# Weight sums staged in place and over several steps, a cosine argument in turns, and earlier re-reads in an attention and two-layer feed-forward kernel

## Chip, cores and metric

The kernel runs on one core of one Trainium2 chip. The metric is device microseconds of one execution, and the median of a few executions is compared. The profiled execution is one more such execution, taken with the hardware profiler; the rows below are its rows.

## What is computed

An attention with a decay, then two feed-forward layers on 2304 tokens of width 512 (the weights arrive as 64-bit floats and are made into pairs of 32-bit parts on the chip):

```python
scores = scale * q @ k.T ; cum = cumsum(log(clip(f)))
scores = where(causal, -1e9, scores + cum[..., :, None] - cum[..., None, :])
x = softmax(scores) @ v                      # 32 heads, 576 x 64 each -> x: 2304 x 512
h = x @ w_in ; x = (h * cos(h)) @ w_out      # first layer, inner width 2048
g = x @ w_gate ; val = x @ w_val             # second layer, inner width 1536
out = (g / (1 + exp(-g)) * val) @ w_out2
```

## The kernel before

Four stages follow each other on the engines. **Attention** (to 191 us of the span) runs by a schedule written out by hand. **The first layer** (191 to 678 us) takes the tokens in 6 chunks of 384 and the inner width in 16 blocks of 128, 96 steps in all (the loop at L691). In a step, TensorE does 12 matmuls of 128x384 into a PSUM tile `h` (`mm_in`, L250) and then the 12 matmuls of `out1` (L613) for the block of two steps earlier. In between, `in1` makes h*cos(h): ScalarE rounds h/2pi+0.25 to an integer `n` (L586), VectorE takes n times 2pi from h in two operations (L590, L592), ScalarE takes the sine (L594), VectorE multiplies (L596), ScalarE casts the product to `gh` (L598) and VectorE takes the rest as `gl` (L116 by `subtract`). `out1` needs both. The order of all this within a step is the string `ORD1`: a digit is an operation of `in1` (5 and 6 are those of the step before), `o` is `out1`, `w` one operation of the conversion of a weight, and `c` one entry of the list `small`. Each engine runs its instructions strictly in the order written, and so does SyncE, which issues all DMAs.

In the same 96 steps the weights are converted. `w_load` (L153) reads a raw weight of 512 KB into one of WRB = 3 buffers `wraw`, `w_step` converts it in five operations (L169 on ScalarE, L171 to L177 on VectorE) into a tile `ta`, and the next raw load is issued behind the fifth. Weights of the first layer get two more operations (L191, L116). The 36 weights of the second layer are taken two at a time by `w_member`, 18 pairs in all: it puts twelve entries on `small`, which are four sums or differences on GpSimd (`tt`, L210, into the one buffer `sums`), and four times a cast to a high part on ScalarE (`high`, L226), a difference on GpSimd for the low part (`low`, L116) and a store of both parts to HBM (L230). High and low part share a tile `wst`, of which there are two. A `c` takes one entry, and where more than TAB2-2 = 2 converted weights are held, `w_step` takes entries off the list at once (L165) until they are fewer.

**The second layer's first half** (678 to 989 us) is done as seven products (a fast 2x2 scheme) per block q of the inner width and per token pass p: two groups of three blocks, three passes each (L878). In a block, `in2` does seven groups of 12 matmuls (L783); VectorE combines them (L676), and `silu` (L763 to L767) makes a 128x384 piece of g four times, once with VectorE and three times with GpSimd, and stores each with three DMAs of 64 KB. During the second block of a pass `x_sums` (L676 on `xb`) combines the inputs of the next pass on VectorE, and during the third `x_split` casts them. `x_read` (L661, four DMAs) re-reads them from HBM; it is called behind the first block of the pass.

**The second layer's second half** (989 to 1149 us) does the same with g: `g_load` (L811) reads it, `g_sums` combines it (GpSimd and VectorE), `g_split` casts it, and `out2` (L842) does seven groups of 18 matmuls for each of nine token tiles t. Tile t+1 is combined and cast during tile t. `g_load(1)` stands behind all reads of the weights (`u_read`, L666).

Of the kernel before, what the change touches and what calls it, by code (L numbers as in the profile page):

```python
# [26 lines left out]
CH = 384  # L27
# [10 lines left out]
TAB = 2  # L38
TAB2 = 4
CHAIN = 1  # L40
# [13 lines left out]
POS_OUT = {2: 0, 3: 1, 5: 2, 6: 3, 7: 4, 4: 5, 1: 6}  # L54
WRB = 3
ORD1 = "0152w634owwccc"
WQ = (3, 2)
# [8 lines left out]
INV2PI = float(1 / (2 * np.pi))  # L66
PI2_HI, PI2_LO = 6.28125, 0.0019353071795864769

# [30 lines left out]
def body(ctx: ExitStack, tc: tile.TileContext, qk, v, f, w_in, w_out, w_gate, w_val, w_out2, mask_c, ident_c, sel_c, out):  # L99
# [6 lines left out]
    x2 = [dram.tile([128, KD, CH], F32, name=f"x2_{k}") for k in range(NC)]  # L106
    w_u = [dram.tile([7, 128, 2, 512], F32, name=f"wu{u}") for u in range(9)]
    g_d = [dram.tile([4, 128, NQ, 128], F32, name=f"gd{t}") for t in range(NIT)]
    r_d = dram.tile([NPAIR, 10, 128], F32, name="r_d")
# [28 lines left out]
    small = []  # L138
    held = [0]

# [15 lines left out]
    def w_step(n, k):  # L156
# [6 lines left out]
        if k == 1:  # L163
            sp = stages[0] if n < SA else stages[1]
            while n >= SB and held[0] > TAB2 - 2:  # L165
                small.pop(0)()
            ta = wcur[n][1] = sp.tile([128, 512], I32, tag="ta", name="ta", bufs=TAB if n < SA else TAB2)
# [30 lines left out]
    def w_member(kind, q):  # L198

        b0, b1 = half.pop((kind, 2 * q)), half.pop((kind, 2 * q + 1))  # L200
        a0, a1, c0, c1 = b0[:, :256], b0[:, 256:], b1[:, :256], b1[:, 256:]
        box = {}
        ins = kind != "p"
        u, mem = (q, "gv".index(kind)) if ins else (NQ + q // 2, q % 2)

        def tt(o, a, b, op):
            if "s" not in box:
                box["s"] = stages[1].tile([128, 4, 256], F32, tag="sums", name="sums", bufs=1)
            a, b = (box["s"][:, x] if isinstance(x, int) else x for x in (a, b))
# [3 lines left out]
        for x in ((0, c0, c1, add), (2, a0, c0, sub), (1, c1, 2, sub), (3, a1, 1, sub)) if ins else \  # L213
                ((2, c1, a1, sub), (0, a1, a0, sub), (1, 2, a0, add), (3, c0, 1, sub)):
            small.append(lambda x=x: tt(*x))
# [346 lines left out]
    lctx = ExitStack()  # L562
    mp2 = lctx.enter_context(tc.tile_pool(name="mp2", bufs=2))
# [3 lines left out]
    stages[1] = rctx.enter_context(tc.tile_pool(name="stage2", bufs=WRB, side=SIDE_R))  # L567
    ps_h = hctx.enter_context(tc.tile_pool(name="ps_h", bufs=3, space=PSUM))

# [6 lines left out]
    def in1(c, j, k):  # L576

        if k == 0:
            h = ps_h.tile([128, 512], F32, tag="h", name="h")[:, :CH]
            mm_in(h, wt["i", j], xs[c])  # L580
            n = mp2.tile([128, CH], I32, tag="n", name="n")
            r = mp3.tile([128, CH], F32, tag="r", name="r")
            hnr[c, j] = h, n, r
        h, n, r = hnr[c, j][:3]
        if k == 1:
            ACT.activation(out=n, in_=h, func=AF.Copy, scale=INV2PI, bias=0.25)  # L586
        elif k == 2:
            a = ps_h.tile([128, 512], F32, tag="a", name="a", bufs=1)[:, :CH]
            hnr[c, j] += (a,)
# [41 lines left out]
    def w_next():  # L631

        n, k = wpos
        if n < len(order):
            w_step(n, k)
        elif n > len(order):
            return
        if k == 5 and n + 1 < len(order):
            w_step(n + 1, 1)
        if SA < n <= SB and k in (3, 4):  # L640
            w_step(n - 1, k + 3)
        if k == 5 and n + WRB < len(order):
            w_load(n + WRB)
        wpos[:] = (n + 1, 2) if k == 5 else (n, k + 1)
# [18 lines left out]
    def u_read(u, i):  # L663
        s, t = slot_tile([128, 2, 2, 256], F32R, "wu")
        wu[u, i] = s, t
        SP.dma_start(out=t.bitcast(F32).rearrange("p m h x -> p m (h x)"), in_=w_u[u][(POS_IN if u < NQ else POS_OUT)[i]])  # L666

# [23 lines left out]
    for i in range(NCH + LAG):  # L691
        if i < NCH:
# [9 lines left out]
            if i == 0:  # L702
                for n in range(WRB):
                    w_load(SA + n)
            if i == WS:
                w_step(SA, 1)
            left = WQ[wpos[0] >= SB and i % 2] if i >= WS else 0
            for k in ORD1:
                if k in "01234":
# [51 lines left out]
    def silu(e, C, g, p, q, blk):  # L761
# [46 lines left out]
    def g_load(t):  # L808
        GT[t] = [slot_tile([128, NQ, 128], F32, "gt") for _ in range(4)]
        for e in range(4):  # L810
            SP.dma_start(out=GT[t][e][1], in_=g_d[t][e])  # L811

# [65 lines left out]
    for st in range(NST):  # L878
        for p in range(NPASS):
            final = st == NST - 1 and p == NPASS - 1  # L880
            nxt = None if final else (p + 1) % NPASS
            for q in range(NQS * st, NQS * st + NQS):
# [13 lines left out]

                in2(p, q, after)
                if k == 0 and not final:
                    for e in range(4):
                        x_read(e, nxt)  # L900
                if k == 0 and p == 0 and st == 0:
                    jobs += [(u, i) for u in range(4, NQ) for i in PO]
            if st == NST - 1 and p == NPASS - 2:
                free.extend(xid.values())
                g_load(0)
                for e in range(3):
                    sums[e] = slot_tile([128, NQ, 128], F32, "gs")
# [74 lines left out]
```

## Time and profile before

| | us |
|---|---|
| median of 3 executions (lowest, highest) | 1150.89 (1150.29, 1151.24) |
| the profiled execution | 1150.39 |
| its span, first to last instruction | 1148.6 |
| TensorE matmul busy in it | 1028.7 (90%) |
| VectorE busy | 720.1 (63%) |
| ScalarE busy | 510.1 (44%) |
| GpSimd busy | 519.0 (45%) |

TensorE is the engine that the others feed. An idle stretch of another engine costs nothing by itself, so the table is read together with the waits of TensorE, and with what its matmuls take when it is not waiting. Its mean granted clock is 0.943 of full speed; the clock has two levels in these rows, 2.4 GHz and half of it.

### The profile page before, as it was taken

The numbers are of one execution on the slowest core, as the hardware profiler recorded it, in microseconds if no ns is written. First come the engines' busy times: TensorE is split into PE (matmuls) and PEld (weight loads), VectorE is DVE, ScalarE is ACT, GpSimd is POOL, SyncE is SP. The second block draws the span as 40 slices with busy tenths as digits, with TensorE's granted clock in tenths as the row PEclk, the third lists the DMA queues.
The fourth block names the chain that finished last, engine by engine and source line by source line (L and its number), as shares of the span: only waits on it lengthen the run. The fifth ranks groups of instructions, "written<-read, shape, count | busy, mean of one in ns | idle before, by whom it ended". The sixth has DMA issues, their size and how long they took to land. (4 is left out here: it accounts for less than half of the span.)

```text
span 1148.6 us, 18643 instructions
## 1 busy us (share of the span) xinstructions
PE 1028.7 (90%) x6728; PEld 977.6 (85%) x6728; DVE 720.1 (63%) x1398; ACT 510.1 (44%) x1112; POOL 519.0 (45%) x476
## 2 busy tenths in 40 slices
PE   7999998999888878878889998989698799869998
PEld 5888886999888778868888998989688799869998
DVE  5888885888776566747655744645445455456763
ACT  7888883555444344434434532322122231324342
POOL 3656553422544545454363104526263546445562
PEclk9999999999988989888889998989898999979999
DMA  5666754234545455544634773134742317944421
GB/s 189 199 178 210 211 172 137 92 120 148 205 151 196 159 170 191 185 165 165 215 108 166 279 245 97 50 97 143 246 125 80 104 42 277 297 145 148 141 98 38
DMA packets 93579, 183.37 MB, mean 160 GB/s; under 512 B 9872, under 2 KB 40880, under 8 KB 93488
## 3 DMA queue, kind: packets, MB, share of 16 engines
q1 hardware_dynamic: 93488, 182.19, 47.5%
q8 instruction: 53, 0.87, 0.3%
q14 instruction: 38, 0.31, 0.1%
HBM read 119.15 MB, written 63.00 MB: 159 GB/s over the span
## 5 line engine op out<-in xcount | busy, mean ns | idle before, releaser
L613 PE MATMUL t<-gh,w 128*128 128x384 f32 x704 | 154.2, 364 | 59.6 <-ACT gh L598 59.4
L613 PEld LDWEIGHTS t<-gh,w 128*128 128x128 f32 x704 | 135.0, 206 | 66.0 <-ACT gh L598 65.3
L783 PE MATMUL b<-c,wu 128*128 128x384 f32 x648 | 131.2, 353 | 33.3 <-DVE u L676 33.3
L250 PE MATMUL h<-xh,w 128*128 128x384 f32 x768 | 155.7, 345 | 0.0
L783 PEld LDWEIGHTS b<-c,wu 128*128 128x128 f32 x648 | 120.9, 201 | 36.6 <-DVE u L676 36.5
L250 PEld LDWEIGHTS h<-xh,w 128*128 128x128 f32 x768 | 142.2, 197 | 0.5 <-issue 0.5
L594 ACT ACTIVATE r<-r,hpi 128x384 f32<-128x384 f32 x96 | 59.2, 616 | 125.9 <-DVE r L592 125.9
L590 DVE SCALAR_TENSOR_TENSOR a<-n,h 128x384 f32<-128x384 int32 x96 | 53.6, 558 | 93.3 <-ACT n L586 93.2
L764 POOL TENSOR_TENSOR s<-u,s 128x384 f32<-128x384 f32 x36 | 40.7, 1131 | 156.8 <-ACT s L763 156.8
L404 ACT ACTIVATE P<-P,mx 128x576 f32<-128x576 f32 (+4 forms) x160 | 87.5, 547 | 4.5 <-DVE mx L397 4.5
L613 PE MATMUL t<-gl,w 128*128 128x384 f32 x352 | 82.7, 360 | 0.0
L783 PE MATMUL c<-c,wu 128*128 128x384 f32 x432 | 82.7, 340 | 0.0
L250 PE MATMUL h<-xl,w 128*128 128x384 f32 x384 | 82.1, 334 | 0.0
L783 PE MATMUL a<-c,wu 128*128 128x384 f32 x432 | 81.3, 335 | 0.2
L763 ACT ACTIVATE s<-u 128x384 f32<-128x384 f32 x36 | 18.8, 523 | 140.5 <-DVE u L676 140.5
L842 PE MATMUL b<-wu,c 128*128 128x256 f32 x486 | 65.4, 290 | 16.0 <-DVE u L676 16.0
L783 PEld LDWEIGHTS c<-c,wu 128*128 128x128 f32 x432 | 77.9, 193 | 0.0
L676 DVE TENSOR_TENSOR u<-b,p 128x768 f32<-128x768 f32 (+1 forms) x54 | 41.8, 775 | 56.3 <-PE b L783 38.8
L397 DVE CUSTOM_DVE_ANT_0 P<-s,mask 128x576 f32<-128x576 f32 (+4 forms) x160 | 68.1, 482 | 14.3 <-PE s L373 14.3
L783 PEld LDWEIGHTS a<-c,wu 128*128 128x128 f32 x432 | 75.1, 188 | 1.8 <-ACT p L787 1.8
L842 PEld LDWEIGHTS b<-wu,c 128*128 128x128 f32 x486 | 61.8, 197 | 16.9 <-DVE u L676 16.4
L171 DVE TENSOR_SCALAR ta<-ta 128x512 f32<-128x512 f32 x68 | 37.2, 548 | 56.4 <-ACT ta L169 56.4
(117 smaller groups left out, 2231.1 us busy)
## 6 DMA issues: line engine op xcount, KB each, us to landing
wu<-wu SPq DMA_DIRECT2D x63, 512.0 KB
wu<-wst SPq DMA_DIRECT2D x54, 512.0 KB
wraw<-in_w_out_dram SPq DMA_DIRECT2D x28, 512.0 KB
gd<-g SPq DMA_DIRECT2D x216, 64.0 KB
gt<-gd SPq DMA_DIRECT2D x36, 384.0 KB
raw<-in_qk_dram SPq DMA_DIRECT2D x16, 576.0 KB
xb<-x SPq DMA_DIRECT2D x24, 384.0 KB
wraw<-in_w_in_dram SPq DMA_DIRECT2D x16, 512.0 KB
```

What stands on the lines that cost most here:

```text
L171: DVE.tensor_scalar(out=ta.bitcast(F32), in0=ta.bitcast(F32), scalar1=HI_MIN, scalar2=HI_MAX, op0=ALU.max, op1=ALU.min)
L250: PE.matmul(ps, lhsT=w[:, a, 128 * kk:128 * kk + 128], rhs=b[:, kk], start=(n == 0), stop=(n == 3 * KD - 1))
L397: DVE.tensor_tensor_reduce(out=view(P[p][:rows, c0:c0 + ext], t), in0=ss[p % 2][:rows, SAT[t][0], SAT[t][1]], in1=view(mask[:rows, m1 - ex ...
L404: ACT.activation(out=o, in_=o, func=AF.Exp, scale=-1.0, bias=mxt[p % 8][:rows, t:t + 1], accum_out=smt[p // 2 % 3][:rows, p % 2, t:t + 1])
L590: DVE.scalar_tensor_tensor(out=a, in0=n, scalar=-PI2_HI, in1=h, op0=ALU.mult, op1=ALU.add)
L594: ACT.activation(out=r, in_=r, func=AF.Sin, bias=hpi, scale=1.0)
L613: PE.matmul(acc[m][:, :CH], lhsT=wo[:, q, 128 * m:128 * m + 128], rhs=x, start=(j == a and n == 0), stop=False)
L676: (e or DVE).tensor_tensor(out=o, in0=a, in1=b, op=op)
L763: ACT.activation(out=s, in_=C[:, 0], func=AF.Sigmoid)
L764: e.tensor_tensor(out=s, in0=C[:, 0], in1=s, op=ALU.mult)
L783: PE.matmul(o[:, mem], lhsT=wu[q, i][1][:, mem, x, 128 * kt:128 * kt + 128], rhs=cmb[i][:, y, kt], start=bool(s and n == 0), stop=(n == 5) ...
L842: PE.matmul(ot, lhsT=cmb[i][:, x, q], rhs=wu[NQ + q // 2, i][1][:, q % 2, y], start=bool(s and n == 0), stop=(n == 3 * NQ - 1), skip_group ...
```

## The change

Three things are changed.

First, the second layer's weights. The low part is now written over the source (`ta` or `sums`) and stored from there, and the high part has a tile `hi` of its own, of which there are four; each is stored by its own DMA, so 144 stores of half the size take the place of 72. The entries of `small` carry the step from which they are due (one to three steps after the pair is complete), and `ORD1` has four `c`, spread over the step, in place of three at its end. Six `ta` tiles and two `sums` take the place of four and one, and two raw buffers that of three.

Second, the cosine's argument: one VectorE operation makes h/(2pi) - n from `h` and `n`, and ScalarE's sine multiplies by 2pi. The second operation and its PSUM tile are gone; `h` has four PSUM tiles, `n` one and `r` two buffers.

Third, the second layer: `x_read` for the next pass is called ahead of `in2` of the first block, each piece of g is stored by one DMA, and `g_load(1)` stands right behind `g_load(0)`, ahead of the reads of the last weights.

```diff
-TAB2 = 4
+TAB2 = 6
+RWB2 = 2
+HIB = 4
-WRB = 3
-ORD1 = "0152w634owwccc"
+ORD1 = "0c152cw64cowwc"
...
     def w_step(n, k):
             while n >= SB and held[0] > TAB2 - 2:
-                small.pop(0)()
+                small.pop(0)[1]()
...
     def w_member(kind, q):
-                box["s"] = stages[1].tile([128, 4, 256], F32, tag="sums", name="sums", bufs=1)
+                box["s"] = stages[1].tile([128, 4, 256], F32, tag="sums", name="sums", bufs=2)
...
+        def later(d, fn, *a):
+            small.append((now[0] + d, lambda: fn(*a)))
...
+        def put(i, h, t):
+            SP.dma_start(out=w_u[u][2 * i:min(2 * i + 2, 7), :, mem, h].rearrange("i p x -> p i x"), in_=t)
+
         def high(i):
-            box[i] = stages[1].tile([128, 2, 2, 256], F32R, tag="wst", name="wst", bufs=2)[:, :2 if i < 3 else 1]
-            ACT.copy(out=box[i][:, :, 0], in_=source(i))
+            box[i] = stages[1].tile([128, 2, 256], F32R, tag="hi", name="hi", bufs=HIB)[:, :2 if i < 3 else 1]
+            ACT.copy(out=box[i], in_=source(i))
 
         def low(i):
-            subtract(POOL, box[i][:, :, 1], source(i), box[i][:, :, 0])
-            SP.dma_start(out=w_u[u][2 * i:min(2 * i + 2, 7), :, mem].rearrange("i p x -> p i x"),
-                         in_=box[i].rearrange("p i h x -> p i (h x)").bitcast(F32))
+            put(i, 0, box[i].bitcast(F32))
+            subtract(POOL, source(i), source(i), box[i])
+            put(i, 1, source(i))
...
-        for i in range(4):
-            small.append(lambda i=i: high(i))
-            small.append(lambda i=i: low(i))
+        for d, f, a in ((1, tt, s[0]), (1, high, (0,)), (1, tt, s[1]), (1, tt, s[2]), (1, tt, s[3]), (1, low, (0,)), (2, high, (3,)), (2, low, (3,)),
+                        (3, high, (1,)), (3, low, (1,)), (3, high, (2,)), (3, low, (2,))):
+            later(d, f, *a)
...
     def in1(c, j, k):
-            DVE.scalar_tensor_tensor(out=a, in0=n, scalar=-PI2_HI, in1=h, op0=ALU.mult, op1=ALU.add)
-        elif k == 3:
-            DVE.scalar_tensor_tensor(out=r, in0=n, scalar=-PI2_LO, in1=hnr[c, j][3], op0=ALU.mult, op1=ALU.add)
+            DVE.scalar_tensor_tensor(out=r, in0=h, scalar=INV2PI, in1=n, op0=ALU.mult, op1=ALU.subtract)
         elif k == 4:
-            ACT.activation(out=r, in_=r, func=AF.Sin, bias=hpi, scale=1.0)
+            ACT.activation(out=r, in_=r, func=AF.Sin, bias=hpi, scale=float(2 * np.pi))
...
-                elif k == "c" and small:
-                    small.pop(0)()
+                elif k == "c" and small and small[0][0] <= i:
+                    small.pop(0)[1]()
...
     def silu(e, C, g, p, q, blk):
-        for m in range(NPASS):
-            SP.dma_start(out=g_d[NPASS * p + m][blk, :, q], in_=g[:, blk, 128 * m:128 * m + 128])
+        SP.dma_start(out=g_d[p][blk, :, :, q], in_=g[:, blk].rearrange("p (m t) -> p m t", m=NPASS))
...
-                in2(p, q, after)
                 if k == 0 and not final:
                     for e in range(4):
                         x_read(e, nxt)
+                in2(p, q, after)
...
                 g_load(0)
                 for e in range(3):
                     sums[e] = slot_tile([128, NQ, 128], F32, "gs")
+                g_load(1)
                 jobs += [(u, i) for i in PO for u in range(NQ, 9)]
...
-    g_load(1)
```

Place 1 is ScalarE in the first layer, over one pair of second-layer weights. L586/L590 makes `n`, L598 `gh`, L594 the sine, L169 the first operation of a weight. Before:

```order
L594 ACTIVATE r<-r,hpi 128x384
L226 CAST wst<-ta 128x2x256
L586 ACTIVATE n<-h 128x384
L598 CAST gh<-h 128x384
L226 CAST wst<-sums 128x2x256 x2
L226 CAST wst<-ta 128x256
L169 ACTIVATE ta<-wraw 128x512
L594 ACTIVATE r<-r,hpi 128x384
L586 ACTIVATE n<-h 128x384
```

And in the changed kernel, over a pair a little later:

```order
L228 CAST hi<-ta 128x512
L594 ACTIVATE r<-r,hpi 128x384
L169 ACTIVATE ta<-wraw 128x512
L590 ACTIVATE n<-h 128x384
L598 CAST gh<-h 128x384
L594 ACTIVATE r<-r,hpi 128x384
L228 CAST hi<-ta 128x256
L228 CAST hi<-sums 128x512
L590 ACTIVATE n<-h 128x384
L598 CAST gh<-h 128x384
L594 ACTIVATE r<-r,hpi 128x384
L228 CAST hi<-sums 128x512
```

The last three casts of a pair stood in a row; now at most two stand together, with `n`, `gh` and the sine of a step between.

Place 2 is SyncE at the first block of a pass of the second layer. `gd` is g in HBM, `xb` the inputs of the next pass. Before, the last stores of the first block, the re-reads and the first stores of the second block:

```order
L767 DMA gd_77<-g 128x128
L767 DMA gd_78<-g 128x128
L661 DMA xb_6960<-x_2_63 128x768
L661 DMA xb_6962<-x_3_64 128x768
L661 DMA xb_6964<-x_2_63 128x768
L661 DMA xb_6966<-x_3_64 128x768
L767 DMA gd_76<-g 128x128
L767 DMA gd_77<-g 128x128
```

Changed, the twelve stores of a whole pass, the re-reads and the twelve stores of the next pass:

```order
L767 DMA gd_76<-g 384x1x128 x12
L661 DMA xb_6858<-x_4_65 128x768
L661 DMA xb_6860<-x_5_66 128x768
L661 DMA xb_6862<-x_4_65 128x768
L661 DMA xb_6864<-x_5_66 128x768
L767 DMA gd_77<-g 384x1x128 x12
```

The re-reads moved from behind the four pieces of the first block to behind the last piece of the pass before.

Place 3 is SyncE around the last pass. Before, `g_load(1)` and `g_load(2)` (tiles `gt`) stood behind the last stores of g, at the end of the first half:

```order
L767 DMA gd_83<-g 128x128
L767 DMA gd_84<-g 128x128
L811 DMA gt_10051<-gd_77 128x768
L811 DMA gt_10052<-gd_77 128x768
L811 DMA gt_10053<-gd_77 128x768
L811 DMA gt_10054<-gd_77 128x768
L811 DMA gt_10059<-gd_78 128x768
```

Changed, `g_load(0)` and `g_load(1)` stand together at the start of the last pass, ahead of the weights `wu` and of that pass's stores:

```order
L767 DMA gd_77<-g 384x1x128 x12
L811 DMA gt_9352<-gd_76 128x768
L811 DMA gt_9353<-gd_76 128x768
L811 DMA gt_9354<-gd_76 128x768
L811 DMA gt_9355<-gd_76 128x768
L811 DMA gt_9363<-gd_76 128x768
L811 DMA gt_9364<-gd_76 128x768
L811 DMA gt_9365<-gd_76 128x768
L811 DMA gt_9366<-gd_76 128x768
L666 DMA wu_9391<-wu_73 128x1024
L666 DMA wu_9406<-wu_74 128x1024
L767 DMA gd_78<-g 384x1x128
```

The second four reads moved ahead by a whole pass.

## Rows read from the trace of the kernel before

**Rows 1.** Busy time by stretch (us, instructions), granted clock, DMA share, GB/s:

```profile
191.00:310.00 119.00, 114.43 (x650) 113.86 (x648) 99.50 (x196) 63.65 (x124) 38.47 (x34) 0.99 0.40 132
310.00:620.00 310.00, 255.00 (x1288) 249.18 (x1289) 192.32 (x361) 134.72 (x271) 152.42 (x163) 0.89 0.49 170
620.00:678.00 58.00, 58.00 (x334) 57.63 (x334) 36.05 (x64) 27.63 (x53) 7.02 (x5) 1.00 0.74 260
...
678.00:989.00 311.00, 277.46 (x1516) 272.56 (x1516) 157.83 (x177) 79.24 (x128) 141.67 (x117) 0.94 0.42 137
989.00:1149.00 160.00, 139.69 (x1132) 138.65 (x1130) 88.86 (x104) 54.00 (x79) 77.21 (x37) 0.94 0.38 130
```

**Rows 2.** Waits of the span: total us, times, longest us:

```profile
ACT wst L226 <- DMA wu<-wst: 81.5, 35, 5.7
...
PE t L613 <- ACT gh L598: 59.4, 17, 5.6
...
PE b L783 <- DVE u L676: 33.3, 10, 8.9
PE b L842 <- DVE u L676: 16.0, 2, 15.7
```

**Rows 3.** Timeline at one wait of the first layer: start, us, [idle before]:

```profile
400.02 5.87 SPq L230 DMA_DIRECT2D wu<-wst  x4
402.88 0.62 ACT L226 CAST wst<-sums 128x512 fp32r<-128x512 f32 x1 [5.75 <-DMA wu<-wst]
...
404.29 0.41 ACT L226 CAST wst<-ta 128x256 fp32r<-128x256 f32 x1 [0.79 <-DMA wu<-wst]
...
405.53 0.47 ACT L598 CAST gh<-h 128x384 fp32r<-128x384 f32 x1
...
406.05 2.93 PE L613 MATMUL t<-gh,w 128*128 128x384 f32 x8 [5.63 <-ACT gh L598]
```

**Rows 4.** Groups by line and shape: busy, mean ns, idle before:

```profile
L592 DVE SCALAR_TENSOR_TENSOR r<-n,a 128x384 f32<-128x384 int32 x96 | 52.1, 543 | 0.0
...
L116 POOL TENSOR_TENSOR wst<-sums,wst 128x512 fp32r<-128x512 f32 x36 | 47.1, 1311 | 51.0 <-ACT wst L226 51.0
...
L169 ACT ACTIVATE ta<-wraw 128x512 f32<-128x512 f32 x68 | 45.6, 670 | 0.0
...
L226 ACT CAST wst<-sums 128x512 fp32r<-128x512 f32 x36 | 22.3, 620 | 59.8 <-DMA wu<-wst 59.5 <-POOL sums L210 0.4
```

**Rows 5.** Timeline at the start of the first layer:

```profile
195.42 2.72 PE L613 MATMUL t<-gh,w 128*128 128x384 f32 x8 [4.17 <-ACT gh L598]
```

**Rows 6.** Timeline of the first pass of the second layer, its second block:

```profile
697.70 1.85 SPq L661 DMA_DIRECT2D xb<-x  x4
...
702.01 0.96 DVE L676 TENSOR_TENSOR xb<-xb,xb 128x768 f32<-128x768 f32 x1 [8.40 <-DMA xb<-x]
...
703.89 4.08 PE L783 MATMUL b<-c,wu 128*128 128x384 f32 x12 [5.03 <-DVE u L676]
```

**Rows 7.** Timeline of the second pass, its first two blocks:

```profile
736.07 2.37 PE L783 MATMUL b<-c,wu 128*128 128x384 f32 x12 [0.73 <-DVE u L676]
736.09 1.01 POOL L765 TENSOR_TENSOR g<-u,s 128x384 f32<-128x384 f32 x1
...
744.73 0.96 DVE L676 TENSOR_TENSOR u<-c,u 128x768 f32<-128x768 f32 x1 [1.12 <-PE c L783]
```

**Rows 8.** Timeline of the second half's first token tile:

```profile
996.06 1.02 POOL L765 TENSOR_TENSOR g<-u,s 128x384 f32<-128x384 f32 x1
...
997.77 2.32 PE L842 MATMUL c<-wu,c 128*128 128x256 f32 x18
...
1000.05 4.52 SPq L811 DMA_DIRECT2D gt<-gd  x8
...
1008.12 1.80 POOL L676 TENSOR_TENSOR gs<-gt,gt 128x768 f32<-128x768 f32 x1 [11.04 <-DMA gt<-gd]
...
1015.79 4.21 PE L842 MATMUL b<-wu,c 128*128 128x256 f32 x18 [15.71 <-DVE u L676]
```

**Rows 9.** The chain that ended last: start, us, work:

```profile
1027.28 2.16 PE a L842 x18
```

More of the change, by code (lines that the diff above doesn't have):

```diff
@@ L66 @@
 INV2PI = float(1 / (2 * np.pi))
-PI2_HI, PI2_LO = 6.28125, 0.0019353071795864769
 QT = [(0, 64, 64, 0), (64, 128, 192, 64), (192, 128, 320, 256), (320, 128, 448, 576), (448, 128, 576, 1024)]
@@ L106, in body @@
     x2 = [dram.tile([128, KD, CH], F32, name=f"x2_{k}") for k in range(NC)]
-    w_u = [dram.tile([7, 128, 2, 512], F32, name=f"wu{u}") for u in range(9)]
-    g_d = [dram.tile([4, 128, NQ, 128], F32, name=f"gd{t}") for t in range(NIT)]
+    w_u = [dram.tile([7, 128, 2, 2, 256], F32, name=f"wu{u}") for u in range(9)]
+    g_d = [dram.tile([4, 128, NPASS, NQ, 128], F32, name=f"gd{p}") for p in range(NPASS)]
     r_d = dram.tile([NPAIR, 10, 128], F32, name="r_d")
@@ L138, in body @@
     small = []
-    held = [0]
+    held, now = [0], [0]
     gsrc = [None]
@@ L212, in w_member @@
         sub, add = ALU.subtract, ALU.add
-        for x in ((0, c0, c1, add), (2, a0, c0, sub), (1, c1, 2, sub), (3, a1, 1, sub)) if ins else \
-                ((2, c1, a1, sub), (0, a1, a0, sub), (1, 2, a0, add), (3, c0, 1, sub)):
-            small.append(lambda x=x: tt(*x))
+        def later(d, fn, *a):
+            small.append((now[0] + d, lambda: fn(*a)))
         def source(i):
@@ L222, in source @@
             return box["s"][:, 2 * i - 2:2 * i]
+        def put(i, h, t):
+            SP.dma_start(out=w_u[u][2 * i:min(2 * i + 2, 7), :, mem, h].rearrange("i p x -> p i x"), in_=t)
         def high(i):
-            box[i] = stages[1].tile([128, 2, 2, 256], F32R, tag="wst", name="wst", bufs=2)[:, :2 if i < 3 else 1]
-            ACT.copy(out=box[i][:, :, 0], in_=source(i))
+            box[i] = stages[1].tile([128, 2, 256], F32R, tag="hi", name="hi", bufs=HIB)[:, :2 if i < 3 else 1]
+            ACT.copy(out=box[i], in_=source(i))
         def low(i):
-            subtract(POOL, box[i][:, :, 1], source(i), box[i][:, :, 0])
-            SP.dma_start(out=w_u[u][2 * i:min(2 * i + 2, 7), :, mem].rearrange("i p x -> p i x"),
-                         in_=box[i].rearrange("p i h x -> p i (h x)").bitcast(F32))
+            put(i, 0, box[i].bitcast(F32))
+            subtract(POOL, source(i), source(i), box[i])
+            put(i, 1, source(i))
             if i == 3:
                 held[0] -= 2
-        for i in range(4):
-            small.append(lambda i=i: high(i))
-            small.append(lambda i=i: low(i))
+        s = ((0, c0, c1, add), (2, a0, c0, sub), (1, c1, 2, sub), (3, a1, 1, sub)) if ins else \
+            ((2, c1, a1, sub), (0, a1, a0, sub), (1, 2, a0, add), (3, c0, 1, sub))
+        for d, f, a in ((1, tt, s[0]), (1, high, (0,)), (1, tt, s[1]), (1, tt, s[2]), (1, tt, s[3]), (1, low, (0,)), (2, high, (3,)), (2, low, (3,)),
+                        (3, high, (1,)), (3, low, (1,)), (3, high, (2,)), (3, low, (2,))):
+            later(d, f, *a)
     def w_slot(n):
@@ L562, in body @@
     lctx = ExitStack()
-    mp2 = lctx.enter_context(tc.tile_pool(name="mp2", bufs=2))
+    mp2 = lctx.enter_context(tc.tile_pool(name="mp2", bufs=1))
     mp3 = lctx.enter_context(tc.tile_pool(name="mp3", bufs=3))
@@ L566, in body @@
     pp = lctx.enter_context(tc.tile_pool(name="pp", bufs=1))
-    stages[1] = rctx.enter_context(tc.tile_pool(name="stage2", bufs=WRB, side=SIDE_R))
-    ps_h = hctx.enter_context(tc.tile_pool(name="ps_h", bufs=3, space=PSUM))
+    stages[1] = rctx.enter_context(tc.tile_pool(name="stage2", bufs=RWB2, side=SIDE_R))
+    ps_h = hctx.enter_context(tc.tile_pool(name="ps_h", bufs=4, space=PSUM))
     G = {}
@@ L581, in in1 @@
             n = mp2.tile([128, CH], I32, tag="n", name="n")
-            r = mp3.tile([128, CH], F32, tag="r", name="r")
+            r = mp2.tile([128, CH], F32, tag="r", name="r", bufs=2)
             hnr[c, j] = h, n, r
-        h, n, r = hnr[c, j][:3]
+        h, n, r = hnr[c, j]
         if k == 1:
@@ L587, in in1 @@
         elif k == 2:
-            a = ps_h.tile([128, 512], F32, tag="a", name="a", bufs=1)[:, :CH]
-            hnr[c, j] += (a,)
-            DVE.scalar_tensor_tensor(out=a, in0=n, scalar=-PI2_HI, in1=h, op0=ALU.mult, op1=ALU.add)
-        elif k == 3:
-            DVE.scalar_tensor_tensor(out=r, in0=n, scalar=-PI2_LO, in1=hnr[c, j][3], op0=ALU.mult, op1=ALU.add)
+            DVE.scalar_tensor_tensor(out=r, in0=h, scalar=INV2PI, in1=n, op0=ALU.mult, op1=ALU.subtract)
         elif k == 4:
-            ACT.activation(out=r, in_=r, func=AF.Sin, bias=hpi, scale=1.0)
+            ACT.activation(out=r, in_=r, func=AF.Sin, bias=hpi, scale=float(2 * np.pi))
         elif k == 5:
@@ L641, in w_next @@
             w_step(n - 1, k + 3)
-        if k == 5 and n + WRB < len(order):
-            w_load(n + WRB)
+        if k == 5 and n + RWB2 < len(order):
+            w_load(n + RWB2)
         wpos[:] = (n + 1, 2) if k == 5 else (n, k + 1)
@@ L665, in u_read @@
         wu[u, i] = s, t
-        SP.dma_start(out=t.bitcast(F32).rearrange("p m h x -> p m (h x)"), in_=w_u[u][(POS_IN if u < NQ else POS_OUT)[i]])
+        SP.dma_start(out=t.bitcast(F32), in_=w_u[u][(POS_IN if u < NQ else POS_OUT)[i]])
     def split_c(i, src):
@@ L702, in body @@
             if i == 0:
-                for n in range(WRB):
+                for n in range(RWB2):
                     w_load(SA + n)
@@ L707, in body @@
             left = WQ[wpos[0] >= SB and i % 2] if i >= WS else 0
+            now[0] = i
             for k in ORD1:
@@ L810, in g_load @@
         for e in range(4):
-            SP.dma_start(out=GT[t][e][1], in_=g_d[t][e])
+            SP.dma_start(out=GT[t][e][1], in_=g_d[t // NPASS][e, :, t % NPASS])
     def g_sums(t, k):
@@ L910, in body @@
     fill()
-    assert not jobs and len(free) == 8, (jobs, free)
-    g_load(1)
+    assert not jobs and len(free) == 4, (jobs, free)
     for t in range(NIT):
```

## The prediction, made before the result was known

> **What bounds the kernel now.** I read three views in this order: busy time by stretch, the waits of TensorE, and the timeline around the longest wait of each kind. The stretch from 620 to 678 us shows the pace of an unhindered TensorE: 334 matmuls of 128x384 in 58.00 us, busy all the time at a granted clock of 1.00 [rows 1], so 0.1737 us each. Against it stand two stretches. From 310 to 620 us 1288 matmuls of the same shape should take 223.7 us and take 310.0: 86.3 us too many, of which 310 - 255 = 55 us are idle and 255.0 - 223.7 = 31.3 us are matmuls at the lower clock, since the mean granted clock falls to 0.89 of 2.4 GHz [rows 1]. From 678 to 989 us 1516 matmuls should take 263.3 us and take 311.0: 47.7 too many. In the last stretch matmuls have 256 columns, 18 of them in 2.16 us [rows 9], so 1132 take 135.8 us and the stretch 160. The waits of TensorE are three kinds: 59.4 us for `gh` in the first layer, 33.3 us and 16.0 us for VectorE in the second [rows 2]. So the kernel is bound by TensorE and by what keeps it waiting, and the question for each part is whether it removes one of these waits.
>
> **Part 1, the weights of the second layer.** The timeline shows how the first kind arises. SyncE issues stores from 400.02; ScalarE's cast into `wst` stands until 402.88 for a store, because there are two such tiles, and the next one until 404.29; `gh` is cast only at 405.53, and TensorE starts at 406.05 after 5.63 us of waiting [rows 3]. ScalarE waited 81.5 us for such stores in 35 places [rows 2]. ScalarE runs in order, so the waiting cast holds up `n`, `gh` and the sine of the step behind it (place 1 of the order). In the change a cast finds one of four tiles, last used by the pair before, whose store was issued some three steps of 24 x 0.174 = 4.2 us earlier. The store took 402.88 - 400.02 = 2.86 us from the issue of its group to the release [rows 3], so ScalarE should not wait at all. That removes 16 of the 17 waits; the first, 4.17 us at 195.42 [rows 5], comes from the start of the layer. What is late next? ScalarE was busy 134.7 of 310 us there, VectorE 192.3 and GpSimd 152.4 [rows 1]; squeezed into 223.7 us that is 60%, 86% (less the removed operation, below) and 68%. None is full, so the whole 86.3 us go. This takes idle and clock together: a clock that fell in the rows did so where TensorE had waited.
>
> What the part adds: 72 more stores. All casts and differences stay in number (0.62 us and 1.31 us [rows 4]), and the difference written over its source is the same operation on the same engine; its price could differ either way, but GpSimd has slack. The DMA queues were busy 0.49 of that stretch and 0.74 in the clean one without hindering TensorE [rows 1], so half-size stores have room. On SyncE a low part's store now waits for GpSimd, and behind it stands the next raw load. With two raw buffers in place of three the load has about 1.6 steps, 6.7 us, to land. Never in 68 times did the first operation wait for it before [rows 4], which proves nothing for two buffers. I take 0, since a ScalarE delay reaches TensorE only when it is longer than the lead of `gh`; in [rows 3] 5.75 + 0.79 us of standing became 5.63 us, so the lead was about 1 us there, of which casts in a row had already used a part. The upper end, a delay of some us at half the 18 pairs, is a rival below.
>
> The Trainium skill speaks against this part: "DMA: Bandwidth & Descriptors", Rules for kernel authors, tells authors to join small transfers into large ones, and its section Anatomy of one DMA gives a fixed cost of about 2.0 us for each DMA (fitted to DMAs issued by GpSimd; these are issued by SyncE). As an estimate by that page, 72 more DMAs would be 144 us if they followed one another. The rows show otherwise: the second release came 404.29 - 402.88 = 1.4 us after the first, half of the 2.86 us of a store, so they overlap [rows 3].
>
> **Part 2, the argument in turns.** It removes 96 VectorE operations of 543 ns, 52.1 us [rows 4]. They are hidden: VectorE is at 62% in the stretch where TensorE waits. The gain on the path is one of them at the start of the layer, 0.5 us of the 4.17 [rows 5]. `n` with one buffer costs nothing, since ScalarE's next `n` stands behind the sine, which needed the read of the old one. In the tighter first layer the removed time is what keeps VectorE from 86%: without 0.54 us a step (54 steps of 4.2 us fill 223.7 us, so 29 us) it is (192.3 - 29) / 223.7 = 73%.
>
> **Part 3, the re-reads.** In the second block of a pass VectorE stands 8.40 us for the re-read `xb`, issued from 697.70, and starts the sum at 702.01, 4.3 us later; behind it the sum of a matmul group is late, and TensorE waits 5.03 us [rows 6]. The reads are late because SyncE stands ahead of them for GpSimd's stores of the first block. Moved ahead, they stand behind the last store of the pass before, which GpSimd makes at 736.09 + 1.01 = 737.1 in the second pass; 4.3 us later, at 741.4, the first sum could start. VectorE comes to it at 744.73 + 0.96 = 745.7 [rows 7]. So 4 us remain, and the stall goes. The third block's short wait of 0.73 us [rows 7], five times, is of another cause (the casts of the new inputs) and stays: 3.7 us. The other five waits are 33.3 - 3.7 = 29.6 us [rows 2]; with the lost clock the stretch gets back 47.7 - 3.7 = 44.0 us. One store for three removes DMA issues from SyncE, which waits anyway: 0.
>
> `g_load(1)`: GpSimd's first sum for tile 1 stood until 1008.12 for a read issued at 1000.05 or later, and TensorE's wait ended at 1015.79, 7.7 us behind the start of that sum [rows 8]. With the read early, GpSimd is free at 996.06 + 1.02 = 997.1; the same 7.7 us end at 1004.8. TensorE's last group before the wait starts at 997.77 and takes 2.16 us [rows 8, 9], so it is ready at 999.9. A wait of 4.8 us is left, with its spell at half clock: the gain is 15.7 - 4.8 = 10.9 us, not 15.7. Four slots fewer make the last weight reads later, by SyncE's order to about 997; their matmuls are the last group of the tile, behind the wait that stays. 0.
>
> **Sum.** 86.3 + 0.5 + 44.0 + 10.9 = 141.7 us off the profiled execution's 1150.4 gives 1008.7. The median before is 0.5 us above that execution, so I say 1009.
>
> **Rivals.** (a) *Raw loads late.* Two buffers, and a load that stands on SyncE behind a store that waits for GpSimd: ScalarE then stands for `wraw` instead of `wst`. For it: fewer buffers, GpSimd's differences of 1.31 us [rows 4] ahead in the queue. Against: half-empty DMA queues. If half of the 86.3 us come back, 1052. (b) *The re-reads still late*, held by the stores of the pass before or by a queue of weight reads: 44 us stay, 1053. The 4 us of margin speak against it. (c) *The last wait goes wholly*, since GpSimd reaches the sum earlier: 4.8 us and about 2 us of clock more, 1002. (d) *Slower: stores in file.* If each of the 72 more stores takes its 2.86 us [rows 3] in the way of the raw load behind it, 72 x 2.86 = 206 us are added: 1215. It decides from 141.7 / 72 = 1.97 us per store on the path. The overlap in [rows 3] and a DMA share of 0.49 [rows 1] speak against it. With the 2.0 us that the Trainium skill gives in "DMA: Bandwidth & Descriptors", Anatomy of one DMA, it would be 1153, as an estimate. (e) *Not what it says:* the casts still come in a run, because the list is emptied at once when more than four weights are held. The 16 waits stay then: 1095. The order shows casts apart (place 1), so I give it little.
>
> **How the numbers follow.** The forecast, 1002 to 1024, gets 0.61 (its upper end leaves 15 us for some small new waits); (a), (b) or parts of them, 1024 to 1060, 0.23; (c), below 1002, 0.05; (e) and larger parts of (a), 1060 to 1148, 0.06; (d) 0.05. The range from 1000 to 1050 leaves out about 0.05 of the forecast's lower side and (c), and some 0.15 above. Faster by over 0.2%, which is about what a measurement of this kernel can tell from no change, is all but (d) and a sliver: 0.94; the same 0.01; slower 0.05.
>
> **What would show it.** In the changed kernel's profile: no wait of a cast into `hi` for a store, one wait of TensorE for `gh` of about 3.6 us, a granted clock of 1.00 from 310 us on to the end of the first layer, which ends near 591 us; no wait of the sums of `xb` for a DMA; five waits of some 0.7 us in the second layer; one of about 5 us in the first tile of `out2`. Waits of L169 for `wraw` would show (a), waits of the sums of `xb` for their reads (b). The prediction is wrong if a new engine fills up in the first layer, GpSimd above all, with its sums, differences and the splits of the next chunk.

## The result and the profile after

The changed kernel takes 1005.62 us (median of 4 executions, 1004.43 to 1007.51) against 1151.07 us for the kernel before beside it: ratio 0.8733, 95% interval 0.8709 to 0.8757. Its profiled execution took 1004.43 us, with a span of 1002.6.

Busy time by stretch of the changed kernel (columns as in rows 1: TensorE matmul, its weight loads, VectorE, ScalarE, GpSimd, granted clock, DMA share, GB/s):

```profile
189.00:310.00 121.00, 119.22 (x688) 118.90 (x688) 96.72 (x180) 67.77 (x136) 47.04 (x41) 1.00 0.43 139
310.00:592.00 282.00, 282.00 (x1626) 281.53 (x1625) 200.45 (x348) 154.39 (x313) 166.99 (x162) 1.00 0.76 244
...
592.00:855.00 263.00, 259.28 (x1481) 255.97 (x1481) 158.34 (x174) 78.44 (x127) 144.70 (x117) 1.00 0.48 162
855.00:1003.00 148.00, 139.22 (x1135) 138.20 (x1133) 89.05 (x105) 54.08 (x79) 77.43 (x38) 0.97 0.37 128
```

From 310 us to past the end of the first layer TensorE is busy all the time: 1626 matmuls in 282 us, 0.1734 us each, the pace that the kernel before reached only in its clean stretch [rows 1]. Waits of the changed kernel (total us, times, longest):

```profile
ACT ta L169 <- DMA wraw<-in_w_val_dram: 6.8, 2, 4.7
ACT ta L169 <- DMA wraw<-in_w_out_dram: 6.6, 3, 2.9
...
PE b L842 <- DVE u L676: 5.0, 2, 4.7
ACT ta L169 <- DMA wraw<-in_w_gate_dram: 4.9, 4, 2.0
...
PE b L783 <- DVE u L676: 3.5, 5, 0.7
...
ACT ta L169 <- DMA wraw<-in_w_in_dram: 2.6, 3, 0.9
...
PE t L613 <- ACT gh L598: 1.8, 1, 1.8
```

TensorE's waits for `gh` went from 59.4 us in 17 places to 1.8 in one, those for VectorE in the first half from 33.3 to 3.5, in the second from 16.0 to 5.0 [rows 2]. No cast waits for a store any more; new are ScalarE's waits for raw weights, 6.8 + 6.6 + 4.9 + 2.6 = 20.9 us in 12 places. The borders of the stages, from the timeline of the changed kernel:

```profile
189.61 0.49 ACT L590 ACTIVATE n<-h 128x384 int32<-128x384 f32 x1 [11.34 <-DMA x<-xp]
...
192.51 1.66 PE L613 MATMUL t<-gh,w 128*128 128x384 f32 x8 [1.78 <-ACT gh L598]
...
586.11 2.24 PE L783 MATMUL a<-c,wu 128*128 128x384 f32 x12
...
863.33 1.84 POOL L676 TENSOR_TENSOR gs<-gt,gt 128x768 f32<-128x768 f32 x1
...
871.03 4.21 PE L842 MATMUL b<-wu,c 128*128 128x256 f32 x18 [4.65 <-DVE u L676]
```

The kernel before ended the first wait at 195.42 [rows 5] and began the second layer at this row of its trace:

```profile
677.83 2.24 PE L783 MATMUL a<-c,wu 128*128 128x384 f32 x12
```

So the 146.0 us of the span (1148.6 to 1002.6) came in three pieces: 195.42 - 192.51 = 2.9 us before the first `gh`; (677.83 - 195.42) - (586.11 - 192.51) = 88.8 us in the first layer; (1148.6 - 677.83) - (1002.6 - 586.11) = 54.3 us in the second. The forecast had 0.5, 86.3 and 54.9. That part of the first piece which is no wait of TensorE, about 0.5 us, is that attention ended earlier in this execution; no run ties it to the change.

### The profile page after: what moved, and what is told of

Same layout as the page of the kernel before. It is cut to its first block, busy times and chain, and to the rows that moved or that the text cites. A ratio compares the mean times of both kernels' runs of the same rounds, so it can differ in the third digit from the quotient of the medians.

```text
span 1002.6 us, 18483 instructions
## 1 busy us (share of the span) xinstructions
PE 982.5 (98%) x6728; PEld 938.5 (94%) x6728; DVE 690.1 (69%) x1302; ACT 505.6 (50%) x1112; POOL 538.2 (54%) x476
## 5 line engine op out<-in xcount | busy, mean ns | idle before, releaser
L613 PE MATMUL t<-gh,w 128*128 128x384 f32 x704 | 136.6, 335 | 1.8 <-ACT gh L598 1.8
L254 PEld LDWEIGHTS h<-xh,w 128*128 128x128 f32 x768 | 134.4, 188 | 0.5 <-issue 0.5
L613 PEld LDWEIGHTS t<-gh,w 128*128 128x128 f32 x704 | 123.1, 188 | 2.6 <-ACT gh L598 2.3
L783 PE MATMUL b<-c,wu 128*128 128x384 f32 x648 | 121.7, 335 | 3.5 <-DVE u L676 3.5
L590 ACT ACTIVATE n<-h 128x384 int32<-128x384 f32 x96 | 47.1, 491 | 143.7 <-PE h L254 132.4
L592 DVE SCALAR_TENSOR_TENSOR r<-h,n 128x384 f32<-128x384 f32 x96 | 53.4, 556 | 95.0 <-ACT n L590 94.6
L783 PEld LDWEIGHTS b<-c,wu 128*128 128x128 f32 x648 | 112.8, 188 | 5.2 <-DVE u L676 5.1
L116 POOL TENSOR_TENSOR w<-ta,w 128x512 fp32r<-128x512 f32 x32 | 44.6, 1395 | 59.4 <-ACT w L191 32.0
L613 PE MATMUL t<-gl,w 128*128 128x384 f32 x352 | 75.2, 334 | 0.0
L254 PEld LDWEIGHTS h<-xl,w 128*128 128x128 f32 x384 | 67.9, 188 | 0.0
```

The costliest lines, as they stand in the source:

```text
L116: eng.tensor_tensor(out=o, in0=a, in1=b.bitcast(F32), op=ALU.subtract)
L254: PE.matmul(ps, lhsT=w[:, a, 128 * kk:128 * kk + 128], rhs=b[:, kk], start=(n == 0), stop=(n == 3 * KD - 1))
L592: DVE.scalar_tensor_tensor(out=r, in0=h, scalar=INV2PI, in1=n, op0=ALU.mult, op1=ALU.subtract)
L613: PE.matmul(acc[m][:, :CH], lhsT=wo[:, q, 128 * m:128 * m + 128], rhs=x, start=(j == a and n == 0), stop=False)
L783: PE.matmul(o[:, mem], lhsT=wu[q, i][1][:, mem, x, 128 * kt:128 * kt + 128], rhs=cmb[i][:, y, kt], start=bool(s and n == 0), stop=(n == 5) ...
```

## The experiments

All times are medians of 4 or 5 executions. The experiments ran in three groups, with the kernel before beside each at 1150.9 to 1151.3 us; the changed kernel's 1005.62 us come from its own group, and differences to it are taken directly.

### The three parts one at a time

*Part 1 alone* is the changed kernel with parts 2 and 3 taken back, except for the buffers of part 2 (four `h`, one `n`, two `r`), which stay. 

> The kernel before with part 1 alone (weight sums in place, spread over steps), with the buffers of part 2 (four h, one n, two r) so that it fits, but the cosine's argument still made by two VectorE operations; the second layer as before. My theory: the first layer loses its 16 waits for gh whatever VectorE does: 1151 - 86 = about 1065 us, no cast into hi waiting for a store, granted clock 1.00 from 310 us to the end of the first layer. Rival (part 2 is needed for it): VectorE at about 86% makes gl or the sine late, waits for gh or gl of several us come back, 1080 us or more.

*Part 2 alone* is the kernel before, with its three `h`, and with this edit:

```diff
...
-            DVE.scalar_tensor_tensor(out=a, in0=n, scalar=-PI2_HI, in1=h, op0=ALU.mult, op1=ALU.add)
-        elif k == 3:
-            DVE.scalar_tensor_tensor(out=r, in0=n, scalar=-PI2_LO, in1=hnr[c, j][3], op0=ALU.mult, op1=ALU.add)
+            DVE.scalar_tensor_tensor(out=r, in0=h, scalar=INV2PI, in1=n, op0=ALU.mult, op1=ALU.subtract)
         elif k == 4:
-            ACT.activation(out=r, in_=r, func=AF.Sin, bias=hpi, scale=1.0)
+            ACT.activation(out=r, in_=r, func=AF.Sin, bias=hpi, scale=float(2 * np.pi))
...
```

> The kernel before with part 2 alone (one VectorE operation less in each step). My theory: the 52 us of VectorE are hidden, 16 waits for gh of the same size stay, 1150 us, within 0.2% of before. Rival (VectorE was part of the cause): casts and products come earlier, the waits shrink, 1140 us or less.

*Part 3 alone* is the kernel before with the re-reads, the stores of g and `g_load(1)` as in the change. 

> The kernel before with part 3 alone (re-reads of x ahead of the stores, one store for each piece of g, g_load(1) with g_load(0)). My theory: 44.0 + 10.9 us go, 1096 us; no sum of xb waits for a DMA, the wait in the first tile of out2 is about 5 us. Rival (re-reads still late without the rest): five waits of 5 us or more stay and the time is 1135 us or more.

| kernel | us (lowest, highest) | ratio, 95% interval | less than before |
|---|---|---|---|
| part 1 alone | 1093.44 (1090.36, 1094.30) | 0.9488, 0.9467 to 0.9510 | 57.5 |
| part 2 alone | 1126.92 (1124.22, 1127.86) | 0.978, 0.976 to 0.980 | 24.0 |
| part 3 alone | 1097.82 (1095.45, 1098.93) | 0.9534, 0.9515 to 0.9554 | 53.1 |
| all | 1005.62 (1004.43, 1007.51) | 0.8733, 0.8709 to 0.8757 | 145.4 |

Part 3 brought what was expected of it. The other two did not: part 1 alone gives two thirds of its 86 us, and the operation that was said to be hidden gives 24 us; both rivals hold. The three gains add up to 134.6 us, 10.8 less than the whole. With part 1 alone no cast waits for a store, and yet TensorE waits in the first layer, for `gh` and for accumulators that VectorE has not yet copied out (`part`):

```profile
PE t L616 <- ACT gh L601: 10.6, 9, 2.6
PE t L616 <- DVE part L626: 4.4, 3, 2.0
PE t L616 <- DVE part L624: 2.3, 1, 2.3
```

Waits of part 2 alone:

```profile
ACT wst L226 <- DMA wu<-wst: 88.6, 35, 5.7
...
PE t L609 <- ACT gh L594: 49.5, 18, 7.3
```

ScalarE stands for stores as long as before (81.5 us in 35 places [rows 2]), but TensorE waits 9.9 us less; the rest of the gain is granted clock: this kernel does 1284 matmuls of the layer at 0.93 in 286 us, the kernel before 1288 at 0.89 in 310 [rows 1].

```profile
310.00:596.00 286.00, 240.84 (x1284) 235.72 (x1285) 166.68 (x306) 134.11 (x271) 160.20 (x163) 0.93 0.52 183
```

### The second VectorE operation put back

The changed kernel with two operations for the argument again, the middle result in `r`. 

> The changed kernel with the two VectorE operations for the cosine's argument put back (the middle result in r in place of the PSUM tile). My theory: 96 operations of some 0.54 us stay hidden even at TensorE's full pace, 1006 to 1008 us. Rival (at full pace VectorE, at 86% by my working, fills up here and there): new waits of TensorE for gh or gl in the first layer, 1015 us or more.

It took 1038.13 us (1036.74 to 1041.23), 32.5 us more than the change: the rival holds. TensorE's waits in the first layer, of which the first, 2.5 us for `gh`, is that at the layer's start:

```profile
PE t L616 <- ACT gh L601: 7.8, 5, 2.5
PE t L616 <- DVE part L626: 5.2, 3, 2.3
...
PE t L619 <- DVE gl L117: 4.1, 4, 1.1
...
PE t L616 <- DVE part L624: 2.3, 1, 2.3
```

The timeline around the end of a chunk shows how (lines in the kernel's own numbering; L595 is the second operation, L619 the `out1` of a chunk's last block, which takes `gl` after two matmuls of `gh`):

```profile
398.62 1.66 PE L616 MATMUL t<-gh,w 128*128 128x384 f32 x8 [2.41 <-ACT gh L601]
...
402.71 1.20 DVE L176 SCALAR_TENSOR_TENSOR ta<-wraw,ta 128x512 int32<-128x512 int32 x1
...
403.84 0.55 DVE L117 TENSOR_TENSOR gl<-h,gh 128x384 fp32r<-128x384 f32 x1
404.31 0.54 DVE L595 SCALAR_TENSOR_TENSOR r<-n,r 128x384 f32<-128x384 int32 x1
404.44 0.44 PE L619 MATMUL t<-gl,w 128*128 128x384 f32 x1 [1.03 <-DVE gl L117]
...
410.15 1.01 DVE L626 COPY part<-t 128x384 f32<-128x384 f32 x2
...
410.85 1.38 PE L616 MATMUL t<-gh,w 128*128 128x384 f32 x3 [2.30 <-DVE part L626]
```

VectorE works from one operation to the next: `gl` stands behind the weight's L176, and the copies that free the accumulators (L626) behind `gl` and the second operation. TensorE waits for `gh`, for `gl` and for a free accumulator: twelve waits at the ends of four chunks, 16.9 us together, and the granted clock falls behind them (0.94 from 385 to 415 us). The other two thirds of each chunk pass without a wait, though VectorE is busy 36.14 of 40 us there:

```profile
345.00:385.00 40.00, 40.00 (x232) 39.83 (x231) 36.14 (x60) 22.13 (x46) 25.33 (x26) 1.00 0.71 219
```

The same stretch of the changed kernel has VectorE at 29.16 of 40:

```profile
345.00:385.00 40.00, 40.00 (x232) 39.82 (x231) 29.16 (x51) 20.67 (x43) 30.54 (x30) 1.00 0.70 215
```

### The load without the longer way

Is it VectorE's load, or the longer way from `h` to `gh`? The changed kernel with an operation on VectorE that nobody reads:

```diff
-ORD1 = "0c152cw64cowwc"
+ORD1 = "0c152cw634cowwc"
...
+        elif k == 3:
+            DVE.scalar_tensor_tensor(out=n.bitcast(F32), in0=n, scalar=INV2PI, in1=n, op0=ALU.mult, op1=ALU.add)
```

> The changed kernel with one VectorE operation added in each step (on 128x384, from n into n, behind the place where the argument is made); its result is read by nothing, so the way from h to gh is as short as in the changed kernel, and VectorE has as much to do as where the two-operation cosine was put back (1038 us). Theory now, after that run: VectorE's queue is full at the ends of the chunks, so the load alone costs the time, 1030 to 1040 us, with TensorE's waits at the same places. Rival: the longer way from h to the sine costs it; then the load alone costs nothing, 1004 to 1010 us.

It took 1024.34 us (1022.48 to 1028.49), between the two, so neither theory holds alone: 18.7 us of the 32.5 come with the load alone. The added operation (L594) takes as long as the one put back (L595 of the kernel before this one), but it writes `n`, so the next `n` waits for it:

```profile
L594 DVE SCALAR_TENSOR_TENSOR n<-n 128x384 f32<-128x384 int32 x96 | 67.1, 699 | 0.0
...
L595 DVE SCALAR_TENSOR_TENSOR r<-n,r 128x384 f32<-128x384 int32 x96 | 64.5, 672 | 0.0
...
ACT n L590 <- DVE n L594: 14.7, 26, 1.1
```

So 18.7 is an upper end for the load, and if the two add up, the other 13.8 us or more belong to the longer way.

### What it is in part 1

*Two tiles `hi`* (`HIB = 2`). 

> The changed kernel with two tiles hi in place of four; casts and sums stay spread over the steps. My theory in the forecast (four tiles end the wait for stores): casts wait again for stores of some 2.9 us and TensorE for gh, 1020 us or more. Rival (the spreading alone suffices, since one to two steps lie between the casts): few waits, 1004 to 1010 us.

*In a row.* The four entries of a step stand at its end and are due at once:

```diff
-ORD1 = "0c152cw64cowwc"
+ORD1 = "0152w64owwcccc"
...
-            small.append((now[0] + d, lambda: fn(*a)))
+            small.append((now[0] + 0 * d, lambda: fn(*a)))
```

> The changed kernel with the four entries for the list in a row at the end of each step, due at once; four tiles hi, six ta, two sums stay. My theory in the forecast (tiles, not spreading): no store is waited for, 1004 to 1012 us. Rival (the spreading is needed): up to two casts and their wait for GpSimd's sums stand ahead of n and gh, TensorE waits for gh in some 18 places, 1025 us or more.

*Both.* 

> The changed kernel with both undone: two tiles hi, and the four entries in a row at the end of each step, due at once (six ta, two sums and the sums in place stay). Theory now: tiles and spreading each cover for the other, so together they cost far more than 9.3 + 6.3 us; casts in a row then wait for stores as before, 1040 to 1074 us (1074 is before with parts 2 and 3: 1127 - 53). Rival: they add up, and the gain of part 1 is due to the six ta and two sums: 1015 to 1025 us.

Two tiles took 1014.90 us (1011.61 to 1016.25), in a row 1011.87 (1009.72 to 1016.78), both 1022.64 (1019.38 to 1025.94): 9.3, 6.3 and 17.0 us more than the change. Two tiles cost less than the theory and more than its rival had; a row at the end of the step costs what the theory allowed; and the two edits nearly add up (9.3 + 6.3 = 15.6), as the last rival had it. With two tiles ScalarE waits for stores in 20 places, yet TensorE hardly does (for `gh` 2.6 us in 3 places, the first wait among them, and for `gl` and the accumulators 3.0 us in 5):

```profile
ACT hi L228 <- DMA wu<-hi: 36.8, 20, 3.6
```

So ScalarE may stand 36.8 us for stores and cost 9. What the two edits take back is 17.0 us of what part 1 gives beside parts 2 and 3, which is near 1126.9 - 53.1 - 1005.6 = 68 us, an estimate that lets the gains of parts 2 and 3 add up. The other 51 or so come from what stayed in all these runs: the low part in place with its own store, six `ta`, two `sums`, two raw buffers, four `c` a step in place of three, and the fourth `h`. Which of these it is was not tried; the fourth `h` is an unlikely one, since TensorE never waits for a free `h` in the kernel before. With both edits ScalarE's waits for stores are still less than half of those of part 2 alone (88.6 us), and TensorE's for `gh` a sixth (49.5):

```profile
ACT hi L228 <- DMA wu<-hi: 40.0, 25, 3.7
...
PE t L613 <- ACT gh L598: 8.1, 6, 2.7
```

### Stores and raw buffers

*Each store as two* of half the size, 288 in place of 144:

```diff
-            SP.dma_start(out=w_u[u][2 * i:min(2 * i + 2, 7), :, mem, h].rearrange("i p x -> p i x"), in_=t)
+            for z in range(2):
+                SP.dma_start(out=w_u[u][2 * i:min(2 * i + 2, 7), :, mem, h, 128 * z:128 * z + 128].rearrange("i p x -> p i x"), in_=t[:, :, 128 * z:128 * z + 128])
```

> The changed kernel with each store of a high or low part made as two stores of half the size, 288 in place of 144. My theory (a store has no price as long as the DMA queues have room): 1004 to 1008 us. Rival (a store costs its time on the path, 2.86 us, or a part of it): 144 x 2.86 = 412 us at worst, 1040 us or more if a tenth of it counts.

It took 1007.89 us (1007.57 to 1011.94): 2.3 us for 144 more stores, 0.016 us each. Rival (d), whose price was 2.86 us each, is out.

*Three raw buffers* (`RWB2 = 3`, with five `ta` and three `hi`). 

> The changed kernel with three raw buffers in place of two (to make room, five ta and three hi in place of six and four). My theory: ScalarE's waits for raw loads (21.0 us in the changed kernel) go, but they never reached TensorE: 1003 to 1008 us. Rival (a) of the forecast: they cost something still, 1000 us or less.

It took 1008.21 us (1007.62 to 1010.56). ScalarE's waits for raw weights are gone and nothing is gained, so rival (a)'s mechanism was there and never reached TensorE: from 310 to 592 us TensorE is busy all the time in both kernels, with 1629 matmuls here and 1626 in the changed kernel. What is lost is at the start of the layer, in the timeline of this kernel:

```profile
185.54 0.33 SPq L482 DMA_DIRECT2D x<-xp  x1
...
191.60 0.49 ACT L590 ACTIVATE n<-h 128x384 int32<-128x384 f32 x1 [13.37 <-DMA x<-xp]
...
194.49 1.97 PE L613 MATMUL t<-gh,w 128*128 128x384 f32 x5 [3.81 <-ACT gh L598]
```

The first `n` waits for the last store of the attention's result (`xp`, L482). In this kernel SyncE issues that store behind three raw loads and `n` starts 6.1 us later (191.60 - 185.54); in the changed kernel it issues it behind two, at this row, and `n` starts 4.0 us later:

```profile
185.59 0.33 SPq L482 DMA_DIRECT2D x<-xp  x1
```

In the kernel before, with three, it is 191.93 - 186.13 = 5.8 us. TensorE waits 3.81 us with three raw loads and 1.78 with two, and from 186 to 200 us its granted clock is 0.76 with three and 1.00 with two. So the third raw load is some 1.8 of the 2.9 us at the start, and the forecast lacked it.

### A faster version

*First step:* the wait that part 3 left in the second half's first tile. The last `silu` stands behind the first sum for tile 1, the split of group 6 behind the sum of group 7.

```diff
...
-                silu(POOL, u2, g, p, q, 1)
+                last = lambda: silu(POOL, u2, g, p, q, 1)
+                if p == NPASS - 1 and q == NQ - 1:
+                    tail.append(last)
+                else:
+                    last()
...
                 if i in PO[:4]:
                     g_sums(t + 1, PO.index(i))
+                if tail:
+                    tail.pop()()
+                if t == 0 and i == 2:
+                    return
+                if t == 0 and i == 7:
+                    g_split(1, 6)
```

> The changed kernel with two moves at the start of the second half: GpSimd makes the first sum for tile 1 ahead of the last product of silu, and the cast and difference of group 6 for tile 1 stand behind the sum that frees TensorE's accumulator. My theory: the 4.65 us wait in the first tile falls to under 1.5 us, and its half-clock spell of some 2 us goes: 999 to 1002 us. Rival (the wait is of the long chain of sums and stays): 1004 us or more.

*Second step:* the split of the last group's input (held in `split3`, `pend`) stands behind the first sum of the next block.

```diff
...
+                    while i == 6 and pend:
+                        pend.pop()()
...
-                    for e in range(4):
+                    for e in range(3):
                         x_read(e, nxt)
+                    pend.insert(0, lambda nxt=nxt: x_read(3, nxt))
+                if k == 0:
+                    pend.extend(split3)
+                    split3.clear()
...
```

> As the run before it, and in the passes of the first half the cast and difference of the last group's input (and the one re-read that overwrites its source) stand behind the first sum of a block. My theory: VectorE's difference of 2.59 us no longer stands ahead of that sum, the five waits of 0.7 us go as well, 996 to 999 us. Rival (another difference takes its place ahead of the sum, or the last group waits for its input): no gain over the run before it, 999 to 1003 us.

The first took 1001.82 us (1000.86 to 1002.64), the second 994.09 (993.89 to 994.26; ratio to before 0.8641, 0.8623 to 0.8659), 11.5 us below the change. The second gained 7.7 us where 3.5 us of waits of the matmuls were to be had. TensorE's groups around one of the five waits, in the first of the two kernels:

```profile
677.51 2.25 PE L783 MATMUL b<-c,wu 128*128 128x384 f32 x12
679.82 2.35 PE L783 MATMUL a<-c,wu 128*128 128x384 f32 x12
682.89 2.38 PE L783 MATMUL b<-c,wu 128*128 128x384 f32 x12 [0.72 <-DVE u L676]
685.11 2.24 PE L783 MATMUL c<-c,wu 128*128 128x384 f32 x12
687.19 2.24 PE L783 MATMUL b<-c,wu 128*128 128x384 f32 x12
```

Undisturbed groups start 2.08 us apart (687.19 - 685.11). Here the distances are 2.31, 3.07 and 2.22: 1.36 us too many for a wait of 0.72, at a granted clock of 1.00. Five of them would be 6.8 us, most of the gain, and the second layer is 6.8 us shorter between the two traces. The waits of TensorE's weight loads, which stand ahead of their matmuls, show what the matmuls' rows leave out:

```profile
PEld b L783 <- DVE u L676: 5.1, 5, 1.0
...
PEld a L783 <- ACT p L787: 1.9, 5, 0.4
```

So in each of the five places two things are late: VectorE's sum, and one group earlier ScalarE's copy of an accumulator (`p`), which stands behind two casts of the split (677.51 us, 1.56 us for both; the copy starts at 678.98). Together they are 7.0 us, and in the second kernel neither wait is left: its copy stands behind one cast there.

## Why the prediction was right, and where it was not

The forecast of 1009 us was 3.4 us too high, and every stage came out within 2.5 us of its term. Its steps fared less evenly than its sum.

- **The pace and the excess.** Right: taking 0.1737 us per matmul as the floor and giving back idle and clock together. The first layer ran at 0.1734, without one stretch at half clock.
- **Part 1, 86.3 us.** The sum over the layer was right, the account of it wrong. The step that failed is "None is full, so the whole 86.3 us go", put down to part 1. Part 1 alone gave 57.5 us: it needs part 2. The shares were estimated well enough: 73% for VectorE in the change (200.45 / 282 = 71%) and 86% with both operations (36.14 / 40 = 90% between the chunks' ends). But with both operations, the rows above show, too little is left at the ends of the chunks, where the copies of the accumulators come on top and `gl` is wanted sooner. That the layer's sum held is in part luck: the change happens to have both parts. By the forecast's prices the kernel without part 2 would take 0.5 us more than the change, and it took 32.5. "ScalarE should not wait at all" was right for stores; that four tiles do it was too simple, since two cost only 9.3 us.
- **Part 2, 0.5 us.** Wrong: 24.0 us alone and 32.5 us at the full pace. The 0.5 us at the start of the layer are there (3.49 us from the first `n` to the first `out1` before, 2.90 after), and they are the small part. "They are hidden" was argued from a mean busy share. The operation lies on the way from `h` to `gh` and it fills an engine that is late at the chunks' ends; at the full pace the run with the idle operation shows both at work. Which of the two gives the 24.0 us alone was not tried.
- **Part 1 and 2 together** are what the forecast called part 1; the 86.8 us of the two stand against 91.7 measured, of which some 1.8 are the third raw load at the start. So the one wait for `gh` that was to be left measured 1.78 us and not 3.6, and the layer ended at 586.1 and not near 591.
- **Stores, raw loads.** Price 0 was right for stores (0.016 us each). For raw loads the lead of `gh` covered 20.9 us of ScalarE's standing: no wait of TensorE came of them. The Trainium skill advises in "DMA: Bandwidth & Descriptors", Rules for kernel authors, to join small transfers, and by the fixed cost of about 2.0 us in its section Anatomy of one DMA, which was fitted to DMAs issued by GpSimd, 144 more stores would be an estimated 288 us in file. The run shows 2.3 us, so that advice does not decide here.
- **Part 3, 44.0 + 10.9 us.** Right: 54.3 in the span and 53.1 alone. The five waits were forecast at 0.73 and measure 0.7; the last wait was forecast at 4.8 and measures 4.65, with the 7.7 us from GpSimd's sum to TensorE that the forecast took over (871.03 - 863.33). The "spell at half clock" behind it came as said: the 18 matmuls at 871.03 take 4.21 us in place of 2.16.
- **The rivals.** (b), (d) and (e) did not come. (a) came as a wait of ScalarE and cost nothing. (c) did not come by itself; made on purpose, it was worth 3.8 us, and not the 6.8 of the forecast, since a wait of 1.47 us stays.

## What to carry to other kernels

A mean busy share does not say that an operation is hidden. Ask where in a period the engine is the last to deliver (here the last block of a chunk, at four of the six chunks) and whether the operation lies on the way to what TensorE waits for; one operation of 0.54 us in each of 96 steps was worth 24.0 us in the kernel before and 32.5 in the changed one. The sum of a stage can be right although its parts are credited wrongly, so take parts apart on the chip before carrying one of them elsewhere.

## What was not expected of the hardware

- Where the matmuls' rows show one wait of 0.72 us, TensorE lost 1.36 us with the granted clock at 1.00. The rows of the weight loads show 1.0 us there and 0.4 us more one group earlier, for another engine; in five places that was 7.0 us, and 6.8 us came back.
- VectorE's difference on 128x768 takes 1.09 us where it starts 0.23 us before one of GpSimd's, and 2.59 us where GpSimd's is under way. In the changed kernel:

```profile
633.01 2.55 POOL L116 TENSOR_TENSOR c<-xb,c 128x768 fp32r<-128x768 f32 x1
...
633.79 2.59 DVE L116 TENSOR_TENSOR c<-xb,c 128x768 fp32r<-128x768 f32 x1
...
636.30 0.94 DVE L676 TENSOR_TENSOR u<-b,p 128x768 f32<-128x768 f32 x1
...
637.30 2.38 PE L783 MATMUL b<-c,wu 128*128 128x384 f32 x12 [0.69 <-DVE u L676]
```

  and in the fastest kernel, where this one of VectorE's begins first:

```profile
633.39 1.09 DVE L116 TENSOR_TENSOR c<-xb,c 128x768 fp32r<-128x768 f32 x1 [1.67 <-ACT c L672]
633.62 2.57 POOL L116 TENSOR_TENSOR c<-xb,c 128x768 fp32r<-128x768 f32 x1
634.92 0.96 DVE L676 TENSOR_TENSOR u<-b,p 128x768 f32<-128x768 f32 x1 [0.45 <-PE b L783]
```

  VectorE's operation ends 0.82 us after GpSimd's (636.38 against 635.56), as if it had stood until then. The Trainium skill's page "SBUF — State Buffer", section Who interferes with whom, describes such a lock for a VectorE instruction with two SBUF inputs beside a GpSimd instruction that reads SBUF; these rows agree with it.
